# A planner's table of durations, the closing branch, the flags and the last output of a fused scan and dense kernel

## The chip, the cores and the metric

The kernel runs on one core of a Trainium2 chip. The time is device microseconds of that core, from launch to end. A core has five engines with a queue of instructions each: TensorE (PE, matrix products), VectorE (DVE), ScalarE (ACT), GpSimd (POOL) and SyncE (SP, which here issues nearly all transfers). Each engine does its instructions in order; between engines they wait for one another by semaphores.

## What is computed

A gated linear scan per head, and behind it a dense layer with a smooth gate:

```python
mag = np.sqrt(a_re * a_re + a_im * a_im)
scale = np.minimum(mag, 0.999) / (mag + 1e-06)
a_re_n, a_im_n = (a_re * scale, a_im * scale)
for t in range(S):
    new_re = ar * S_re - ai * S_im
    new_im = ar * S_im + ai * S_re
    S_re, S_im = (new_re + kv, new_im)          # kv = k[t] v[t]^T
    y[:, :, t] = np.einsum('bhd,bhde->bhe', q[:, :, t], S_re)
...
h = x @ w_in                                    # x = y as 3072 tokens x 384
g = np.where(pos, h, np.where(neg, 0.0, (h + beta) ** 2 / (4.0 * beta)))
return (g @ w_out).astype(np.float32)
```

There are 4 batches, 8 heads, 768 steps and a head size of 48 in float32; w_in is 384 x 2048, w_out 2048 x 384.

## The kernel before

The 3072 tokens are cut into 12 units of 256, and the units into 6 blocks of 2. For each unit, `gates(u)` turns the gate inputs into running sums, logarithms, angles and exponentials (DVE and ACT, with triangular sums on PE in the head of the program), and multiplies them into x (for q) and kq (for k). `spread` moves these into the tiles hd by DMAs on SP (pieces of 288, 128 and 32 KB). `attend(u)` then does the scan as chunked attention on PE: scores, transposes, values and products, bundled in visits, with DVE copying masked scores into am and ACT copying results. Results go to xr, with small moves from partition to partition (`move`, 16 KB). `split(blk)` makes a high part xH (ACT) and a low part xL (DVE) of x.

`moe(blk)` does the dense layer of 512 tokens: for each of 16 slices f of the hidden size a `gemm1` (h, 9 matmuls of 128x512: three groups of three) and a `gemm2` (9 matmuls into the three outputs o, again three groups). Between them s (ACT), g (DVE), gh (ACT, a rounded copy) and gl (DVE, the rest) are made of h. In the trace o's three banks are o_112, o_113 and o_114. At a block's end ACT copies o to ob, and SP sends it.

The weights come in a coded form (raw_i, raw_o) and are decoded by `weights`: integer operations on DVE (y_i, y_o, raw_i, raw_o), casts on ACT, and for the first ones a pair of matmuls (rest) on PE. The fast path is valid only within bounds of the inputs, so `slopes` and `ranges` (tiles far and chk) accumulate checks on ACT; in the last block these are 32 operations of 128x768 on chk.

No order is written by hand. All of this are operations of a `Plan`, each with an engine, a planned duration, what it reads and writes, and for some a due time. `Plan.order` simulates the engines with those durations (and LAT, the hand-over between engines; DMA_FIX and a rate for transfers; LANES transfers at a time) and picks for each engine what goes next; the program has that order on each engine. `emit(warm)` puts idle matmuls (L1293) on PE where the plan has PE waiting before the dense layer begins.

After the planned part, written by hand: DVE reduces the accumulated checks to flags (L1334 to L1342), PE adds them over the partitions (L1346), DVE makes `ok` of them (L1348, L1350), every engine loads `ok` into a register (L1353), and a branch on it (L1354) leaves out a slow path for inputs outside of the bounds. The code of that path lies between the branch and the end of the program.

## Time and profile before

| what | value |
|---|---|
| median of 3 runs | 576.93 us (575.53 to 577.64) |
| the profiled execution, time | 578.44 us |
| the profiled execution, span | 576.7 us |
| mean granted clock of PE | 0.994 |
| first matmul of the dense layer | 69.05 us |
| last matmul of the dense layer starts | 568.76 us |

The span runs from the first to the last instruction of the profile, and all times below are microseconds from its start. Busy is the time in which an engine executes; an arrow in a row names what an engine waited for, with the us of idle time before it. Rows whose engine ends in q show the sequencer's own instructions (branches, register loads, issues of DMAs), which aren't counted as busy. PE's granted clock is 1.00 at full rate.

### The profile page before, as it was taken

The numbers are of one execution on the slowest core, as the hardware profiler recorded it, in microseconds if no ns is written. First come the engines' busy times: TensorE is split into PE (matmuls) and PEld (weight loads), VectorE is DVE, ScalarE is ACT, GpSimd is POOL, SyncE is SP. The second block draws the span as 40 slices with busy tenths as digits, with TensorE's granted clock in tenths as the row PEclk, the third lists the DMA queues.
The fourth block names the chain that finished last, engine by engine and source line by source line (L and its number), as shares of the span: only waits on it lengthen the run. The fifth ranks groups of instructions, "written<-read, shape, count | busy, mean of one in ns | idle before, by whom it ended". The sixth has DMA issues, their size and how long they took to land.

```text
span 576.7 us, 10719 instructions
## 1 busy us (share of the span) xinstructions
PE 560.3 (97%) x4284; PEld 466.6 (81%) x4284; DVE 438.9 (76%) x610; ACT 391.0 (68%) x636; POOL 4.1 (1%) x27
## 2 busy tenths in 40 slices
PE   8999889999999999999999999999999999999994
PEld 8788768878888888888888888888887888888883
DVE  6999889899969998887887878887666644454453
ACT  7777678988975857776667486666355543369972
POOL 2000000000000000000000000000000000000000
PEclk9999989999999999999999999999999999999998
DMA  8678371863541602614403414403553500087721
GB/s 352 277 209 265 110 243 60 254 228 109 159 166 42 200 27 57 211 56 117 150 2 101 167 56 117 151 2 90 179 165 97 171 1 8 19 308 254 258 92 61
DMA packets 23673, 80.59 MB, mean 140 GB/s; under 512 B 4544, under 2 KB 10304, under 8 KB 23616
## 3 DMA queue, kind: packets, MB, share of 16 engines
q1 hardware_dynamic: 23616, 79.84, 41.7%
q8 instruction: 35, 0.57, 0.4%
q14 instruction: 22, 0.18, 0.1%
HBM read 55.05 MB, written 4.72 MB: 104 GB/s over the span
## 4 chain that ended last, share of the span: by engine, by line
PE 75%; DVE 11%; DMA 5%; ACT 4%; issue 2%; SPq 1%; ACTq 0%; DVEq 0%
PE h L1165 29%; PE o L1240 29%; PE at L992 5%; PE at L1044 3%; PE at L1036 3%; PE at L961 2%; DMA far<-in_ari_dram 2%; PE at L932 2%; ACT ai L626 2%; SPq L420 1%; DVE x L836 1%; DMA raw_i<-in_wl_dram 1%; DVE kq L836 1%; DVE raw_i L458 1%; DMA ai<-in_art_dram 1%
## 5 line engine op out<-in xcount | busy, mean ns | idle before, releaser
L1165 PE MATMUL h<-xH,wi 128*128 128x512 f32 x576 | 181.3, 396 | 4.5 <-DVE g L1209 3.0
L1240 PE MATMUL o<-gh,wo 128*128 128x512 f32 x576 | 180.2, 394 | 0.0
L1165 PEld LDWEIGHTS h<-xH,wi 128*128 128x128 f32 x576 | 105.9, 188 | 27.7 <-DVE g L1209 3.8
L1240 PEld LDWEIGHTS o<-gh,wo 128*128 128x128 f32 x576 | 106.3, 188 | 22.2 <-issue 0.3
L1165 PE MATMUL h<-xL,wi 128*128 128x512 f32 x288 | 112.8, 392 | 0.4 <-DVE xL L1142 0.4
L1240 PE MATMUL o<-gl,wo 128*128 128x512 f32 x288 | 112.4, 390 | 0.0
L1209 DVE TENSOR_TENSOR g<-h,s 128x512 f32<-128x512 f32 x96 | 65.9, 686 | 56.3 <-ACT s L1190 44.6
L1223 ACT CAST gh<-g 128x512 fp32r<-128x512 f32 x96 | 59.3, 617 | 53.3 <-DVE g L1217 51.0
L1190 ACT ACTIVATE s<-h,cst 128x512 f32<-128x512 f32 x96 | 65.5, 683 | 38.2 <-PE h L1165 35.6
L1227 DVE TENSOR_TENSOR gl<-g,gh 128x512 fp32r<-128x512 f32 x96 | 65.8, 686 | 32.8 <-ACT gh L1223 32.4
L1165 PEld LDWEIGHTS h<-xL,wi 128*128 128x128 f32 x288 | 54.2, 188 | 12.8 <-DVE xL L1142 1.1
L1240 PEld LDWEIGHTS o<-gl,wo 128*128 128x128 f32 x288 | 54.1, 188 | 11.8 <-DVE gl L1227 0.2
L1217 DVE SCALAR_TENSOR_TENSOR g<-s,g 128x512 f32<-128x512 f32 x80 | 55.3, 691 | 2.3
L626 ACT ACTIVATE ai<-ai 128x768 f32<-128x768 f32 x48 | 40.3, 843 | 20.1 <-DMA ai<-in_ari_dram 8.8
L992 PEld LDWEIGHTS at<-hd 96*64 96x64 f32 x704 | 33.2, 140 | 7.8 <-issue 6.3
L992 PE MATMUL at<-hd 96*64 96x64 f32 (+1 forms) x704 | 37.1, 255 | 0.0
L701 DVE TENSOR_TENSOR_SCAN ai<-again,ai 128x768 f32<-128x768 uint8 x20 | 35.0, 1751 | 0.3
L1044 PE MATMUL at<-am,V 128*64 128x128 f32 x352 | 32.9, 273 | 0.0
L1004 DVE COPY_PREDICATED am<-tri,at 128x512 f32<-128x512 uint32 x44 | 31.6, 737 | 1.6 <-PE at L992 1.6
L1036 PE MATMUL at<-hd,st 96*64 96x128 f32 x304 | 30.5, 278 | 0.3 <-DVE am L1004 0.3
L1293 PE MATMUL idle<-tri,ident 128*128 128x128 f32 x204 | 27.1, 292 | 1.8 <-POOL tri masks.py:66 1.8
L1293 PEld LDWEIGHTS idle<-tri,ident 128*128 128x128 f32 x204 | 26.3, 208 | 2.7 <-POOL tri masks.py:66 1.8
(124 smaller groups left out, 643.3 us busy)
## 6 DMA issues: line engine op xcount, KB each, us to landing
chk<-in_wl_dram SPq DMA_DIRECT2D x16, 768.0 KB, 6.4
kq<-in_kq_dram SPq DMA_DIRECT2D x12, 768.0 KB, 5.8
ai<-in_ari_dram SPq DMA_DIRECT2D x10, 768.0 KB, 6.2
V<-in_v_dram SPq DMA_DIRECT2D x12, 576.0 KB, 4.1
hd<-x SPq DMA_DIRECT2D x24, 288.0 KB, 3.7
hd<-kq SPq DMA_DIRECT2D x24, 288.0 KB, 4.0
raw_i<-in_wl_dram SPq DMA_DIRECT2D x8, 768.0 KB, 7.0
raw_o<-in_wl_dram SPq DMA_DIRECT2D x8, 768.0 KB, 4.7
```

The source lines that it names most:

```text
L626: lambda: A_.activation(out(), src(), f, **kw),
L992: PE_.matmul(SC.get()[o : o + HC, i + e, HC * k :], t[:, 0, ks], t[:, 1, qs], start=True, stop=True,)
L1036: PE_.matmul(o_, st.get().rearrange("p h e -> p (h e)")[:, lo : lo + 64], head(h)[:, 1, cs], start=True, stop=False,)
L1044: PE_.matmul(o_, V.get()[:, c, lo : lo + 64], ams[pr // 2].get()[:, 2 * (pr % 2) + e, :], start=st is None, stop=True,)
L1165: PE_.matmul(H.get(), weight["i", f // 2].get()[:, f % 2, part, sl], x.get()[:, j, :], start=j == 0 and n == 0, stop=j == NJ - 1 and n == 2,)
L1190: lambda: A_.activation(SS.get(), H.get(), AF.Relu, bias=c_half, scale=-0.5 if spare else 0.5),
L1209: lambda: V_.tensor_tensor(G.get(), H.get(), SS.get(), op=ALU.max),
L1217: lambda: V_.scalar_tensor_tensor(G.get(), SS.get(), 1.0, G.get(), op0=ALU.min, op1=ALU.mult),
L1223: pl.op("ACT", act(T), lambda: A_.copy(GH.get(), G.get()), r=[G], w=[GH])
L1227: lambda: V_.tensor_tensor(GL.get(), G.get(), GH.get().bitcast(F32), op=ALU.subtract),
L1240: PE_.matmul(PO[m].get(), weight["o", f // 2].get()[:, f % 2, part, sl], g.get(), start=f == 0 and n == 0, stop=f == NF - 1 and n == 2,)
L1293: PE_.matmul(idle["h1"], ident, mask, start=True, stop=True)
```

## The change

Four things are changed.

*The planner's table.* Transfers have a little less fixed cost; moves between tiles have constants of their own and a duration by size in place of a rate; transposes, products, scores and values have other planned durations; 400 ns at the head of a values visit go, and the last part of a visit has 300 or 100 ns added in place of 90. Nothing computed changes by it, but the order of the operations does, on every engine.

*The end of the last block.* With `BACK = 3`, gemm2 of f = 13, 14 and 15 is held back in the last block and done output by output, and gemm1 of f = 15 is due 0.6 of a step earlier. The last output, m = 2, is copied in two halves of 256 columns, one by ACT and one by DVE, and sent by two transfers, one on ACT's queue and one on SP's.

*Flags.* They become planned operations: they are on DVE as soon as all operations that accumulate checks (`marks`) are done, PE's sum stands ahead of o of f = 13, and `ok` is made ahead of gl of f = 15. The register loads of SP, ACT, DVE and POOL are planned as well and stand ahead of the last output's copies and transfers; PE's comes last. `nc.snap` replaces `nc.values_load` and does without two small instructions on SP (FUSED_REGOPS and SEQ_ASSERT).

*The branch.* `mark_branch_hint_location` puts one BRANCH_PREFETCH_HINT at the beginning of every engine's program, which names the closing branch and says that it is likely taken.

```diff
-DMA_FIX, DMA_END, DMA_ISSUE, LANES = 2400, 50, 470, 8
-LOAD, MOVE = 410.0, 240.0
+DMA_FIX, DMA_END, DMA_ISSUE, LANES = 2350, 50, 440, 8
+MOVE_FIX, MOVE_ISSUE = 1750, 605
+LOAD = 410.0
+MOVE = {16: 180, 32: 185, 128: 360, 288: 1330}
...
+BACK = 3
...
-                own = DMA_FIX + DMA_END + dma + 600
+                own = self.fix[i] + DMA_END + dma + 600
...
-                q.append(max(t + DMA_FIX, q[-1]) + dma)
+                q.append(max(t + self.fix[i], q[-1]) + dma)
...
+QUEUES = {
+    mybir.EngineType.SP: "SP",
+    mybir.EngineType.Activation: "ACT",
+    mybir.EngineType.DVE: "DVE",
+    mybir.EngineType.Pool: "POOL",
+}
...
-    def dma(nbytes, dst, src, r=(), w=(), due=None, rate=LOAD, eng="SP", after=()):
+    def dma(nbytes, dst, src, r=(), w=(), due=None, move=False, eng="SP", after=()):
         queue = {"SP": nc.sync, "ACT": nc.scalar, "POOL": nc.gpsimd}[eng]
         return pl.op(
             eng,
-            DMA_ISSUE,
+            MOVE_ISSUE if move else DMA_ISSUE,
             lambda: queue.dma_start(dst(), src()),
             r=r,
             w=w,
-            dma=nbytes / rate,
+            dma=MOVE[nbytes // 1024] if move else nbytes / LOAD,
             due=due,
             after=after,
+            fix=MOVE_FIX if move else DMA_FIX,
         )
...
+    def mark(*args, **kw):
+        marks.append(pl.op(*args, **kw))
...
-        pl.op(
+        mark(
             "ACT",
             act(N, acc=True) + 50,
             lambda: A_.activation(
...
-            ve(80, lambda: V_.tensor_copy(dst, A()[:, :, U - 1]), [a], [STATE[0]])
+            marks.append(ve(80, lambda: V_.tensor_copy(dst, A()[:, :, U - 1]), [a], [STATE[0]]))
...
-                out.append((4 * 83, run, [hd[h // 3] for h in GROUPS[g]], TP, tail))
+                out.append((4 * 76, run, [hd[h // 3] for h in GROUPS[g]], TP, tail))
...
-            return [(NH * 124, run, [*kT, V_c[0]], DP, tail)]
+            return [(NH * 114, run, [*kT, V_c[0]], DP, tail)]
...
-                out.append((2 * 340, run, [hd[h // 3] for h in GROUPS[g]], SC, tail))
+                out.append((2 * 345, run, [hd[h // 3] for h in GROUPS[g]], SC, tail))
...
-                return ((4 if st else 2) * len(prs) * 110 + (400 if prs[0] == 0 else 0), run, r, Y, tail)
+                return ((4 if st else 2) * len(prs) * 113, run, r, Y, tail)
...
+            mode = not 300 < parts[0][0] < 310
             last = None
             for n, (cost, run, r, psum, tail) in enumerate(parts):
-                cost += 90 if n == len(parts) - 1 else 0
+                if n == len(parts) - 1:
+                    cost += 300 if mode else 100
...
-                    due=t0 + STEP * (f + j / 6),
+                    due=t0 + STEP * (f + j / 6 - 0.6 * (f + 1 == NF and held_back > 0)),
...
+            gated.append(i)
+
+        def gemm2(f, ms=range(NJ), late=0.0):
+            GH, GL = gs[f]
+            for m in ms:
...
+                    due=t0 + STEP * (f + LAG - 0.5 + late + m / 6),
...
+        held_back = BACK if blk == NBLK - 1 else 0
         for k in range(NF + LAG):
             if k < NF:
                 gemm1(k)
-            if k >= LAG:
+            if LAG <= k < NF + LAG - held_back:
                 gemm2(k - LAG)
+        for m in range(NJ if held_back else 0):
+            for f in range(NF - held_back, NF):
+                gemm2(f, (m,), NF - f - 1 + (m * held_back + f) / 9)
...
+            due = t0 + STEP * (NF + LAG + 1.5)
+            ends = blk == NBLK - 1 and m == NJ - 1
+            for n, eng in enumerate(("ACT", "DVE") if ends else ("ACT",)):
+                sl = slice(n * U, (n + 1) * U) if ends else slice(0, T)
+                us = BLOCKS[blk][n : n + 1] if ends else BLOCKS[blk]
+                slot = "y" if n else turn_of("s", 3)
+                OB = tl(slot, [P, sl.stop - sl.start], F32, f"ob_{blk}_{m}_{n}")
+                copy = A_.copy if eng == "ACT" else V_.tensor_copy
+                i = pl.op(
+                    eng,
+                    act(sl.stop - sl.start, psum=True),
+                    lambda m=m, OB=OB, sl=sl, copy=copy: copy(OB.get(), PO[m].get()[:, sl]),
+                    r=[PO[m]],
+                    w=[OB],
+                    due=due,
+                )
+                if blk < NBLK - 1:
+                    finals.append(i)
+                dma(
+                    P * (sl.stop - sl.start) * 4,
+                    lambda m=m, us=us: out[PLACE[us[0]] : PLACE[us[-1]] + 1 : NPART, m].rearrange(
+                        "n p t -> p n t"
+                    ),
+                    lambda OB=OB: OB.get().rearrange("p (n t) -> p n t", t=U),
+                    r=[OB],
+                    due=due + STEP / 2,
+                    eng="ACT" if ends and n == 0 else "SP",
+                )
...
+    for fn in (
+        lambda: V_.tensor_scalar(fsum[:, 0], fsum[:, 0], SUM, None, op0=ALU.is_le),
...
+        lambda: V_.tensor_reduce(ok4[:, 3:4], wall, axis=AX.X, op=ALU.min),
+    ):
+        pl.op("DVE", 150, fn, w=[OK], after=marks, due=BEGIN[NBLK])
+    pl.op("PE", 190, lambda: PE_.matmul(FP.get(), ones, ok4, start=True, stop=True), r=[OK], w=[FP])
+    pl.op("DVE", 150, lambda: V_.tensor_reduce(ft, FP.get(), axis=AX.X, op=ALU.add), r=[FP], w=[OK])
+    pl.op(
+        "DVE",
+        150,
+        lambda: V_.tensor_scalar(ok, ft, 4.0 * P, None, op0=ALU.is_equal),
+        w=[OK],
+    )
+    for reg in regs:
+        if reg.engine in QUEUES:
+            pl.op(
+                QUEUES[reg.engine],
+                1000,
+                lambda reg=reg: nc.reg_load(reg, ok[0:1, 0:1]),
+                r=[OK],
+                after=[gated[-1]],
+                due=BEGIN[NBLK],
+            )
+
     with tc.manual_schedule():
+        tc.mark_branch_hint_location("general", "LikelyTaken", engines=mybir.ALL_ENGINES)
         pl.emit(warm)
-
...
+        for reg in regs:
+            if reg.engine not in QUEUES:
+                nc.reg_load(reg, ok[0:1, 0:1])
     fast.close()
 
-    within = nc.values_load(ok[0:1, 0:1], min_val=0, max_val=1)
-    with tc.If(within == 0):
+    within = nc.snap(regs, donate=True, min_val=0, max_val=1)
+    with tc.If(within == 0, label="general"):
```

How the order moves, at three places. (A number behind a tile's name counts the program's tiles; before and after, the same tile has another number.)

DVE in the head, where the products with kq of the first two units (kq_129 and kq_137) are made; raw_i_141 and raw_o_257 are weights. Before:

```order
L836 TENSOR_TENSOR x_139<-kq_129,ai_124 128x1536
L788 TENSOR_SCALAR state<-ai_126 128x3
L836 TENSOR_TENSOR kq_129<-kq_129,ai_124 128x1536
L458 SCALAR_TENSOR_TENSOR raw_i_141<-raw_i_141,y_i_294 128x768
L836 TENSOR_TENSOR x_146<-kq_137,ai_126 128x1536
L467 SCALAR_TENSOR_TENSOR raw_i_141<-raw_i_141 128x768
L836 TENSOR_TENSOR kq_137<-kq_137,ai_126 128x1536
L449 TENSOR_SCALAR y_o_382<-raw_o_257 128x768
L458 SCALAR_TENSOR_TENSOR raw_o_257<-raw_o_257,y_o_382 128x768
```

After, the same weights are raw_i_149 and raw_o_248; the four products (L852 now) come four rows and more behind these:

```order
L462 TENSOR_SCALAR y_i_290<-raw_i_149 128x768
L471 SCALAR_TENSOR_TENSOR raw_i_149<-raw_i_149,y_i_290 128x768
L480 SCALAR_TENSOR_TENSOR raw_i_149<-raw_i_149 128x768
L771 TENSOR_SCALAR ai_132<-o_114 128x512
L779 SCALAR_TENSOR_TENSOR ai_132<-o_114,ai_132 128x512
L771 TENSOR_SCALAR ai_132<-at_111 128x256
L779 SCALAR_TENSOR_TENSOR ai_132<-at_111,ai_132 128x256
L804 TENSOR_SCALAR state<-ai_132 128x3
L462 TENSOR_SCALAR y_o_317<-raw_o_248 128x768
```

The integer work on raw_i_149 and the first operation on the next weight (y_o) stand ahead of the products, rather than among and behind them.

DVE at the first h of the dense layer: x_342 and kq_492 are the products of unit 2, xL_681 the low part that the first h reads, and wo, y_i and raw_i weights. Before:

```order
L836 TENSOR_TENSOR x_342<-kq_492,ai_144 128x1536
L1142 TENSOR_TENSOR xL_681<-xr_467,xH_675 128x256
L836 TENSOR_TENSOR kq_492<-kq_492,ai_144 128x1536
L1142 TENSOR_TENSOR xL_681<-xr_467,xH_675 128x256 x2
L640 TENSOR_TENSOR ai_499<-ai_499 128x768
L478 TENSOR_TENSOR wo_753<-raw_o_534,wo_753 128x2x384
L449 TENSOR_SCALAR y_i_774<-raw_i_584 128x768
L458 SCALAR_TENSOR_TENSOR raw_i_584<-raw_i_584,y_i_774 128x768
L467 SCALAR_TENSOR_TENSOR raw_i_584<-raw_i_584 128x768
L1209 TENSOR_TENSOR g_0_792<-h_0_737,s_0_776 128x512
```

After (kq_512, xL_682; x_361 stands just ahead of it):

```order
L852 TENSOR_TENSOR kq_512<-kq_512,ai_152 128x1536
L1161 TENSOR_TENSOR xL_682<-xr_488,xH_671 128x256 x2
L989 TENSOR_TENSOR st_647<-st_647,o_112 96x384
L1161 TENSOR_TENSOR xL_682<-xr_488,xH_671 128x256
L656 TENSOR_TENSOR ai_518<-ai_518 128x768
L480 SCALAR_TENSOR_TENSOR raw_i_530<-raw_i_530 128x768
L1228 TENSOR_TENSOR g_0_806<-h_0_765,s_0_793 128x512
```

Of the four operations on weights between xL and the first g (L1209, now L1228) one is left there, and all of xL comes behind the product kq.

PE at the end of the program, from the first o on that reads gh of f = 14 (before) and of f = 15 (after). Before:

```order
L1240 MATMUL o_112<-gh_14_5293,wo_1574 128x512 x2
L1240 MATMUL o_112<-gl_14_5298,wo_1574 128x512
L1240 MATMUL o_113<-gh_14_5293,wo_1574 128x512 x2
L1240 MATMUL o_113<-gl_14_5298,wo_1574 128x512
L1240 MATMUL o_114<-gh_14_5293,wo_1574 128x512 x2
L1240 MATMUL o_114<-gl_14_5298,wo_1574 128x512
L1240 MATMUL o_112<-gh_15_5320,wo_1574 128x512 x2
L1240 MATMUL o_112<-gl_15_5325,wo_1574 128x512
L1240 MATMUL o_113<-gh_15_5320,wo_1574 128x512 x2
L1240 MATMUL o_113<-gl_15_5325,wo_1574 128x512
L1240 MATMUL o_114<-gh_15_5320,wo_1574 128x512 x2
L1240 MATMUL o_114<-gl_15_5325,wo_1574 128x512
```

After, where gh_13_5286, gh_14_5315 and gh_15_5338 belong to f = 13, 14 and 15:

```order
L1260 MATMUL o_112<-gh_15_5338,wo_1602 128x512 x2
L1260 MATMUL o_112<-gl_15_5344,wo_1602 128x512
L1260 MATMUL o_113<-gh_14_5315,wo_1602 128x512 x2
L1260 MATMUL o_113<-gl_14_5322,wo_1602 128x512
L1260 MATMUL o_113<-gh_15_5338,wo_1602 128x512 x2
L1260 MATMUL o_113<-gl_15_5344,wo_1602 128x512
L1260 MATMUL o_114<-gh_13_5286,wo_1514 128x512 x2
L1260 MATMUL o_114<-gl_13_5294,wo_1514 128x512
L1260 MATMUL o_114<-gh_14_5315,wo_1602 128x512 x2
L1260 MATMUL o_114<-gl_14_5322,wo_1602 128x512
L1260 MATMUL o_114<-gh_15_5338,wo_1602 128x512 x2
L1260 MATMUL o_114<-gl_15_5344,wo_1602 128x512
```

Six groups of three follow from the first o of f = 15 on, rather than three, and the last three groups all go into one output.

More of the change, by code (lines that the diff above doesn't have):

```diff
@@ L137, in tile, with op @@
         return t
-    def op(self, eng, cost, fn, r=(), w=(), due=None, dma=0, after=(), glue=None):
+    def op(self, eng, cost, fn, r=(), w=(), due=None, dma=0, after=(), glue=None, fix=DMA_FIX):
         i = len(self.ops)
@@ L526, in ranges @@
         )
-        pl.op(
+        mark(
             "ACT",
@@ L622, in ac @@
             cost = act(N, ptr=not isinstance(kw.get("bias", 0.0), float), acc=acc_ is not None)
-            pl.op(
+            (pl.op if acc_ is None else mark)(
                 "ACT",
@@ L855, in spread @@
                     r=[t],
-                    rate=MOVE,
+                    move=True,
                     eng=eng,
@@ L865, in spread @@
                     r=[t],
-                    rate=MOVE,
+                    move=True,
                     eng=eng,
@@ L876, in spread @@
                         r=[t],
-                    rate=MOVE,
+                    move=True,
                     eng=eng,
@@ L1075, in move @@
                     r=[(XR, (x, ub * U + q * CH)) for q in range(NC) for x in (False, True)],
+                    move=True,
                     w=[(XR, (ub, e, j))],
@@ L1231, in gemm1 @@
             gs[f] = (GH, GL)
-        def gemm2(f):
-            GH, GL = gs.pop(f)
-            for m in range(NJ):
+            gated.append(i)
+        def gemm2(f, ms=range(NJ), late=0.0):
+            GH, GL = gs[f]
+            for m in ms:
                 def mms(m=m):
@@ L1325, in gated_scan_moe @@
         moe(blk)
+    ok4 = const.tile([P, 4], F32, name="ok4")
+    ft = const.tile([1, 1], F32, name="ft")
+    ok = const.tile([1, 1], mybir.dt.int32, name="ok")
+    regs = nc.alloc_registers("within", engines=mybir.ALL_ENGINES)
+    wall = wsum.rearrange("p a b -> p (a b)")
+    decs = fdec.rearrange("p a b -> p (a b)")
+    OK, FP = fixed(ok4), tl("at0", [1, 4], F32, "fp")
+    for fn in (
+        lambda: V_.tensor_scalar(fsum[:, 0], fsum[:, 0], SUM, None, op0=ALU.is_le),
+        lambda: V_.tensor_reduce(ok4[:, 0:1], fsum[:, 0], axis=AX.X, op=ALU.min),
+        lambda: V_.tensor_scalar(fsum[:, 1], fsum[:, 1], FOURTH, None, op0=ALU.is_le),
+        lambda: V_.tensor_reduce(ok4[:, 1:2], fsum[:, 1], axis=AX.X, op=ALU.min),
+        lambda: V_.tensor_scalar(decs, decs, DECAY, None, op0=ALU.is_lt),
+        lambda: V_.tensor_reduce(ok4[:, 2:3], decs, axis=AX.X, op=ALU.min),
+        lambda: V_.tensor_scalar(wsum[:, 0], wsum[:, 0], T_SUM, None, op0=ALU.is_le),
+        lambda: V_.tensor_scalar(wsum[:, 1], wsum[:, 1], 0.0, None, op0=ALU.is_le),
+        lambda: V_.tensor_reduce(ok4[:, 3:4], wall, axis=AX.X, op=ALU.min),
+    ):
+        pl.op("DVE", 150, fn, w=[OK], after=marks, due=BEGIN[NBLK])
```

50 lines of the change are left out of this document (7 added, 43 removed).

## The prediction

> **What bounds the kernel now.** I read the page first, then the waits of PE, the busy time by stretches, and the timeline of the last 20 us. Page: the busy time of the engines, and the shares of the chain that ended last.
>
> ```profile
> span 576.7 us, 10719 instructions
> ...
> PE 560.3 (97%) x4284; PEld 466.6 (81%) x4284; DVE 438.9 (76%) x610; ACT 391.0 (68%) x636; POOL 4.1 (1%) x27
> ...
> PE 75%; DVE 11%; DMA 5%; ACT 4%; issue 2%; SPq 1%; ACTq 0%; DVEq 0%
> ```
>
> PE is busy for 97% of the span, so only idle time of PE, work added to it, and the time before its first and after its last useful matmul can move the end. Busy time by stretches (from:to, length, then each engine's busy us):
>
> ```profile
> 60.00:80.00 20.00, 15.49 (x136) 12.39 (x135) 17.16 (x24) 15.78 (x26) 0.00 (x0) 0.96 0.49 149
> 100.00:560.00 460.00, 459.30 (x3306) 380.31 (x3305) 345.35 (x474) 310.54 (x516) 0.00 (x0) 1.00 0.39 126
> ```
>
> From 100 to 560 us PE lacks 0.7 us of being full: a better order can gain no more than that there, though it can lose. What is left lies at three places: the head (before the dense layer's first matmul at 69.05), the turn from 60 to 80 us, where 20.00 - 15.49 = 4.5 us of PE are idle, and the end. The two largest waits of PE that the change can reach, the nearest row for a wait on attention, and the timeline of the first and third h:
>
> ```profile
> PE h L1165 <- DVE g L1209: 3.0, 2, 2.6
> PE h L1165 <- ACT xH L1135: 1.6, 1, 1.6
> PE at L1036 <- DVE am L1004: 0.3, 1, 0.3
> ```
> ```profile
> 69.05 0.73 PE L1165 MATMUL h<-xH,wi 128*128 128x512 f32 x2 [1.59 <-ACT xH L1135]
> ...
> 76.85 0.73 PE L1165 MATMUL h<-xH,wi 128*128 128x512 f32 x2 [2.58 <-DVE g L1209]
> ```
>
> **The end** is the largest term. Timeline of the last matmuls and outputs, the issues of the output's transfers (KB each, us to landing), and the instructions of the closing branch (count, shortest/median/longest in ns, first and last start):
>
> ```profile
> 566.25 0.69 DVE L1227 TENSOR_TENSOR gl<-g,gh 128x512 fp32r<-128x512 f32 x1 [0.69 <-ACT gh L1223]
> ...
> 566.86 0.17 DVE L1334 TENSOR_SCALAR fsum<-fsum 128x12 f32<-128x12 f32 x1
> ...
> 567.40 0.39 PE L1240 MATMUL o<-gl,wo 128*128 128x512 f32 x1
> ...
> 567.88 1.89 ACT L1267 COPY ob<-o 128x512 f32<-128x512 f32 x3 [1.67 <-PE o L1240]
> ...
> 568.50 1.67 SPq L420 DMA_DIRECT2D out_dram<-ob  x3
> ...
> 568.76 0.39 PE L1240 MATMUL o<-gl,wo 128*128 128x512 f32 x1
> ```
> ```profile
> out_dram<-ob SPq DMA_DIRECT2D x3, 256.0 KB, 2.3
> ```
> ```profile
> L1353 PEldq TENSOR_LOAD <-ok x1: 603/603/603, 569.7 to 569.7; - x1
> ```
> ```profile
> L1354 SPq EVENT_SEMAPHORE  x8: 17/17/17, 574.8 to 575.3; - x8
> L1354 ACTq COMPARE_BRANCH  x1: 50/50/50, 570.2 to 570.2; - x1
> L1354 POOLq COMPARE_BRANCH  x1: 45/45/45, 570.4 to 570.4; - x1
> L1354 PEldq COMPARE_BRANCH  x1: 4744/4744/4744, 570.4 to 570.4; - x1
> ...
> L1354 POOLq EVENT_SEMAPHORE  x1: 17/17/17, 570.8 to 570.8; - x1
> ...
> L1354 ACTq EVENT_SEMAPHORE  x1: 17/17/17, 574.3 to 574.3; - x1
> ```
>
> The last matmul starts at 568.76 and the span ends at 576.7: 7.9 us. The branch over the fallback is where they go. POOL is past it in 0.4 us (570.4 to 570.8); ACT needs 4.1 (570.2 to 574.3), PE 4.7. The page counts 27 instructions on POOL and 610 to 4284 on the others, so I read the 4 us as the fetch of code that is not at hand, where POOL's still is. If the announcement makes it there, every engine is past in POOL's 0.4 us, and the last output decides: its copy begins 0.4 us after the last matmul's start (three copies of 0.63 end at 567.88 + 1.89 = 569.77, the last begins at 569.14); half a copy takes 0.3 to 0.6, I take 0.4, its transfer starts at once and lands 2.3 later, so 568.76 + 0.4 + 0.4 + 2.3 = 571.9. Behind it stand the closing waits, 574.8 to 576.7 = 1.9 us; about half of them need not wait for the landing. The end is then 572.8 to 573.8, I take 573.2: **-3.5 us** (bounds -2.9 and -3.9). The early flags and register loads are in it: with them nothing but the output is late, and without the flags the 0.6 us of the load would stand in front of PE's branch. If the branch still fetches, PE's load and branch begin 0.6 us earlier and nothing else: -0.6.
>
> [...]
>
> **The last block's order.** ACT and DVE make one pair gh, gl per 2.7 us there, and the first can't be earlier, since ACT goes from its checks straight to s of f = 13:
>
> ```profile
> 557.05 1.00 ACT L530 ACTIVATE chk<-chk,cst 128x768 f32<-128x768 f32 x1
> ...
> 558.04 0.66 ACT L1190 ACTIVATE s<-h,cst 128x512 f32<-128x512 f32 x1
> 560.19 0.62 ACT L1223 CAST gh<-g 128x512 fp32r<-128x512 f32 x1 [1.48 <-DVE g L1217]
> 560.71 0.68 ACT L1190 ACTIVATE s<-h,cst 128x512 f32<-128x512 f32 x1
> ```
>
> gl of f = 15 ends at 566.25 + 0.69 = 566.94, and the matmul that first reads it stands at 567.40, a slack of 0.46 us. Now six groups rather than three follow from o0 of f = 15 on. A group of three matmuls takes 0.68 us (567.40 to 568.76 is two of them), so that PE comes there 3 x 0.68 = 2.04 us sooner, though gl comes no sooner: it waits 2.04 - 0.46 = 1.6 us. Nine flag operations like the fsum row (0.17 us) now stand among g and gl on DVE, mostly in gaps like the 0.69 of the gl row; with the flag's matmul on PE I add 0.1. **+1.7 us**, bounds +0.5 (ACT done with its checks a us sooner) and +2.3 (all flag work on the chain).
>
> **The head.** DVE, where it now has the weights' integer work ahead of the attention's, and PE's first groups:
>
> ```profile
> 9.86:32.31 22.45, 20.82 (x31) 1.00 0.74 296
> ...
> 67.57:76.19 8.62, 8.55 (x12) 1.00 0.61 174
> ```
> ```profile
> 32.31 1.76 DVE L836 TENSOR_TENSOR kq<-kq,ai 128x1536 f32<-128x1536 f32 x1
> 33.99 0.95 DVE L458 SCALAR_TENSOR_TENSOR raw_i<-raw_i,y_i 128x768 uint32<-128x768 uint32 x1
> ...
> 36.52 0.95 DVE L467 SCALAR_TENSOR_TENSOR raw_i<-raw_i 128x768 uint32<-128x768 uint32 x1
> ...
> 39.06 0.56 DVE L449 TENSOR_SCALAR y_o<-raw_o 128x768 uint32<-128x768 uint32 x1
> ...
> 69.57 1.75 DVE L836 TENSOR_TENSOR kq<-kq,ai 128x1536 f32<-128x1536 f32 x1
> ```
>
> The second to fourth row pass the product that ends kq of the first unit (32.31): 0.95 + 0.95 + 0.56 = 2.5 us more ahead of it. DVE idles 22.45 - 20.82 = 1.6 us before it, and about 1 of that is filled, since the weights' loads also go ahead of kq on SP. So the first scores come 1.5 us later. Up to the first g DVE does the same set of work in both orders, and is then without a gap (8.55 of 8.62); what was moved ahead is not done behind. The third h, which waits for that g, is therefore 0 to 1.5 us later; I take **+1.0**. The hint as second instruction of SP adds at most 0.1, in the bounds.
>
> **The middle** is local: a visit of attention goes ahead of or behind one group of the dense layer. With 0.7 us to gain and more to lose, **+0.5**, bounds -0.7 and +2.
>
> **The clock.** Windows of 3.41 us laid on the edges of the half-clock stretch: length, PE busy, granted clock:
>
> ```profile
> 68.12:71.53 3.41, 2.31 (x8) 1.00 0.36 98
> ...
> 74.95:78.36 3.41, 1.51 (x7) 1.00 0.74 181
> 78.36:81.77 3.41, 3.41 (x30) 0.50 0.96 387
> ```
>
> One stretch with PE busy for 1.51 of 3.41 us cost the next one half its clock, 1.7 us of work; 2.31 did not. The new order puts the second product of unit 2 (the 1.75 us at 69.57) ahead of all of xL rather than behind its first piece, so that the first h comes 1.0 + 1.75 = 2.75 us later where the third is only 1.0 later, and the wait of 2.58 at the third h shrinks to 0.8 at least; I take 1.4, since the wait for xL inside the first two h goes as well. That leaves 2.0 busy in any such stretch, between the two rows and nearer to the upper; where a stretch's edge falls inside the wait it is more. I take the dip to be gone: **-1.7**, bound 0.
>
> **Sum.** -3.5 + 1.7 + 1.0 + 0.5 - 1.7 = -2.0 us. The profiled execution took 578.44 (its span is 576.7), which is 1.5 above the median of the runs, 576.93; the difference is taken off the median: **574.9 us**. 0.5%, or 2.9 us, is about what a measurement of this kernel can tell from no change, so that "faster" begins below 574.0.
>
> **Rivals.**
> 1. Good ends: the tail's wait is short (+0.5), head and middle cost nothing, the dip goes: -3.5 + 0.5 - 1.7 = -4.7, 572.2 us. For it: DVE's total in the head is unchanged. Against: the slack of 0.46 before six groups. Chance 0.26.
> 2. The announcement does nothing and the branch still fetches: -0.6 in place of -3.5, 577.8 us, no change. For it: it stands hundreds of instructions ahead of the branch. Against: only the not yet fetched code explains 4.1 against 0.4 us. Chance 0.13.
> 3. Slower: the attention's values now come too early. For a visit that begins with values the planner held 400 + 90 ns beyond its matmuls and now holds 300, so that what follows is fitted in closer; PE runs in order, so that a visit whose masked scores are not yet copied stops everything behind it.
>
> ```profile
> L1004 DVE COPY_PREDICATED am<-tri,at x44: 706/736/762, 42.3 to 477.8; 128x512 f32<-128x512 uint32 x44
> ```
>
> Two copies a visit, with the four into another bank, are 24 visits. A wait of 0.3 us (the one in the row of waits) at each is 7 us: 574.9 + 7 = 582. It turns the sign at 576.93 - 574.9 = 2.0 us, 0.08 a visit, and is slower by over 0.5% from 4.9 us, 0.2 a visit. Against: groups of the dense layer that don't depend on them stand between most of these, and the waits of PE have one single wait for am in the whole run. Chance 0.11.
>
> **Chances.** My forecast 0.5, the rivals 0.26, 0.13, 0.11. Faster by over 0.5%: the first rival and the lower edge of my own case, 0.34. Slower: 0.11. Same: 0.55. The range goes from the first rival, 572.0, past the second to 579.0; beyond are most of the third and a little below.
>
> **What would show it.** Branch: ACT's and PE's next instruction within 0.6 us of theirs, and 4 to 5 us from the last matmul to the end; a PE branch of over 4 us is rival 2. Tail: a new wait of PE for gl or g of 1 to 2 us in the last 15 us. Head: first h at 70 to 72 us, its third f about 1 us later than 76.85. Clock: no stretch at 0.50 after 70 us. Middle: under 2 us of PE idle from 100 to 560; many waits for am there is rival 3. I am wrong if the head is earlier, or if the last output's landing takes well over 3 us.

## The result, and the profile after

| kernel | median | runs | ratio to before, 95% interval |
|---|---|---|---|
| before | 578.12 us (575.53 to 579.61) | 8 | |
| after | 580.91 us (579.21 to 584.88) | 8 | 1.0052 [1.003, 1.0074] |

The changed kernel is slower by 0.5%; 574.9 us were predicted, with 572.0 to 579.0 as range. The forecast stood on a median of three runs for before, 576.93; with eight it is 578.12, so that 1.2 us of the 6.0 between 574.9 and 580.91 belong to the baseline: as a change, -2.0 us were forecast and +2.8 measured. The profiled execution of after took 579.93 us (span 578.1) against 578.44 (span 576.7), so that the profile shows about half of the difference; the other half is looked for in the profiles of the experiments.

The page of after, and the busy time by stretches (from:to, length, busy us of PE, PEld, DVE, ACT and POOL, granted clock, DMA share, GB/s), and below them the row of before for 100 to 200 us:

```profile
span 578.1 us, 10750 instructions
...
PE 561.2 (97%) x4300; PEld 466.0 (81%) x4300; DVE 439.1 (76%) x611; ACT 391.2 (68%) x636; POOL 4.1 (1%) x27
```
```profile
60.00:80.00 20.00, 17.53 (x185) 14.95 (x181) 16.59 (x24) 15.22 (x25) 0.00 (x0) 1.00 0.48 135
100.00:200.00 100.00, 96.42 (x707) 78.74 (x706) 88.06 (x117) 80.24 (x123) 0.00 (x0) 1.00 0.49 152
100.00:560.00 460.00, 456.30 (x3288) 377.12 (x3287) 343.21 (x473) 309.30 (x514) 0.00 (x0) 1.00 0.39 125
```
```profile
100.00:200.00 100.00, 99.69 (x727) 82.42 (x726) 90.89 (x122) 83.82 (x129) 0.00 (x0) 1.00 0.51 162
```

From 60 to 80 us PE is busy for 17.53 us where it was 15.49, but that is hardly progress: 0.9 us of it is idle matmuls (5.59, was 4.70), and a step of the attention ahead of the dense layer (the transposes with ident) comes 2.0 us later (61.00, was 58.97), so that more of it falls into this stretch. What is better is the clock: before ran at half of it for 3.4 us from 78.4 on, after does not. The middle is worse: 460.00 - 456.30 = 3.7 us of PE idle from 100 to 560, where it was 0.7, and nearly all of it between 100 and 200 us. PE's waits, and the third h in the timeline:

```profile
PE h L1184 <- DVE g L1228: 3.7, 4, 1.7
...
PE at L948 <- DVE am L1020: 1.2, 2, 0.8
PE o L948 <- DVE am L1020: 1.0, 1, 1.0
```
```profile
76.89 0.73 PE L1184 MATMUL h<-xH,wi 128*128 128x512 f32 x2 [1.75 <-DVE g L1228]
...
117.15 0.74 PE L1184 MATMUL h<-xH,wi 128*128 128x512 f32 x2 [0.48 <-DVE g L1228]
...
122.31 0.73 PE L1184 MATMUL h<-xH,wi 128*128 128x512 f32 x2 [0.75 <-DVE g L1228]
...
128.13 0.55 PE L948 MATMUL at<-ident,hd 96*128 96x96 f32 x4 [0.76 <-DVE am L1020]
...
161.61 1.52 PE L1008 MATMUL at<-hd 96*64 96x128 f32 x30 [0.89 <-DMA hd<-kq]
...
179.42 0.73 PE L1184 MATMUL h<-xH,wi 128*128 128x512 f32 x2 [0.71 <-DVE g L1228]
```

The third h comes when it did (76.89, was 76.85), after a shorter wait. The new waits are five: for g at 117, 122 and 179 us, for am at 128, and for a move (hd<-kq) at 161.6; they make 3.6 us. What holds g at 117 and 122 us is on DVE. First before, then after, the timeline of DVE (in brackets the idle time ahead and what ended it), and SP's issues in after:

```profile
112.83 0.95 DVE L640 TENSOR_TENSOR ai<-ai 128x768 f32<-128x768 f32 x1
115.61 0.56 DVE L449 TENSOR_SCALAR y_i<-raw_i 128x768 uint32<-128x768 uint32 x1 [1.83 <-DMA raw_i<-in_wl_dram]
116.09 0.68 DVE L1209 TENSOR_TENSOR g<-h,s 128x512 f32<-128x512 f32 x1
```
```profile
111.32 0.95 DVE L656 TENSOR_TENSOR ai<-ai 128x768 f32<-128x768 f32 x1
115.93 0.56 DVE L462 TENSOR_SCALAR y_i<-raw_i 128x768 uint32<-128x768 uint32 x1 [3.66 <-DMA raw_i<-in_wl_dram]
116.41 0.69 DVE L1228 TENSOR_TENSOR g<-h,s 128x512 f32<-128x512 f32 x1
```
```profile
103.84 1.80 SPq L432 DMA_DIRECT2D hd<-x  x3
105.74 0.68 SPq L432 DMA_DIRECT2D hd<-kq  x1
107.10 0.35 SPq L447 DMA_DIRECT2D raw_i<-in_wl_dram  x1
107.51 1.16 SPq L432 DMA_DIRECT2D hd<-kq  x2
```

In both kernels the decoding of a weight (y_i) stands ahead of g on DVE, and the weight lands at nearly the same time, 115.6 and 115.9. In after the s that g reads is done on ACT at 112.70 (112.07 + 0.63), and g starts at 116.41, right behind y_i, though DVE idled for 3.66 us. After is 1.5 us earlier there (ai at 111.32, was 112.83), which is about the 1.7 us that PE did not lose to a half clock at 78 us, and DVE waits 1.8 us longer: so much of a gain is given back at one load, and 1.2 us of it shows as idle PE at 117 and 122 us. The wait for am at 128 us follows the next weight in the same way (DVE waits 0.70 us for raw_o at 125.29). The other two, 1.6 us, do not stand behind a decoding: at 161.6 PE waits for a move itself, and the g of 179 us stands on DVE behind a product with kq (177.02 to 178.7). In after the load of 116 us, of 768 KB, is issued at 107.10 behind four moves and ahead of six, and lands after 8.8 us; in before it is issued at 108.96 behind six and ahead of four, and lands after 6.6. For a load with nothing queued ahead of it the planner holds 2350 + 768 x 1024 / 410 + 50 ns = 4.3 us.

The end. The closing branch (count, shortest/median/longest in ns, first and last start), the last two copies, the last transfers (KB, us to landing), and SP's closing semaphores:

```profile
L1404 PEldq COMPARE_BRANCH  x1: 391/391/391, 569.5 to 569.5; - x1
...
L1404 ACTq COMPARE_BRANCH  x1: 68/68/68, 573.6 to 573.6; - x1
...
L1404 ACTq EVENT_SEMAPHORE  x1: 17/17/17, 574.1 to 574.1; - x1
```
```profile
572.82 0.37 ACT L1298 COPY ob<-o 128x256 f32<-128x256 f32 x1 [1.41 <-PE o L1260]
...
573.23 0.42 DVE L1298 COPY ob<-o 128x256 f32<-128x256 f32 x1 [4.44 <-ACT ob L1298]
```
```profile
out_dram<-ob ACTq DMA_DIRECT2D x1, 128.0 KB, 2.0
out_dram<-ob SPq DMA_DIRECT2D x1, 128.0 KB, 2.9
```
```profile
L1635 SPq EVENT_SEMAPHORE  x10: 17/28/28, 576.8 to 578.1; - x10
```

The last matmul starts at 572.40 and the span ends at 578.1: 5.7 us, where it was 7.9. ACT is past its branch in 0.5 us (573.6 to 574.1). But the halves don't run beside each other: DVE's copy waits for ACT's (573.23 is behind 572.82 + 0.37), and its transfer is the one that lands last.

### The profile page after: what moved, and what is told of

Read it like the earlier page. It is cut to its first block, busy times and chain, and to the rows that moved or that the text cites. A ratio compares the mean times of both kernels' runs of the same rounds, so it can differ in the third digit from the quotient of the medians.

```text
span 578.1 us, 10750 instructions
## 1 busy us (share of the span) xinstructions
PE 561.2 (97%) x4300; PEld 466.0 (81%) x4300; DVE 439.1 (76%) x611; ACT 391.2 (68%) x636; POOL 4.1 (1%) x27
## 4 chain that ended last, share of the span: by engine, by line
PE 63%; DMA 15%; DVE 11%; ACT 8%; issue 2%; SPq 1%; ACTq 0%; DVEq 0%
PE o L1260 24%; PE h L1184 24%; PE at L1008 5%; DMA chk<-in_wl_dram 4%; PE at L1052 3%; PE at L1060 3%; DMA hd<-kq 2%; PE at L977 2%; ACT chk L546 2%; PE at L948 2%; DMA raw_i<-in_wl_dram 2%; DMA kq<-in_kq_dram 1%; SPq L432 1%; DMA out_dram<-ob 1%; DVE g L1228 1%
## 5 line engine op out<-in xcount | busy, mean ns | idle before, releaser
L1228 DVE TENSOR_TENSOR g<-h,s 128x512 f32<-128x512 f32 x96 | 66.0, 687 | 55.9 <-ACT s L1209 44.4
L1209 ACT ACTIVATE s<-h,cst 128x512 f32<-128x512 f32 x96 | 65.5, 682 | 38.8 <-PE h L1184 36.2
L1008 PE MATMUL at<-hd 96*64 96x128 f32 (+1 forms) x704 | 36.7, 251 | 0.9 <-DMA hd<-kq 0.9
```

Of the source, the lines that this page charges most:

```text
L1008: PE_.matmul(SC.get()[o : o + HC, i + e, HC * k :], t[:, 0, ks], t[:, 1, qs], start=True, stop=True,)
L1209: lambda: A_.activation(SS.get(), H.get(), AF.Relu, bias=c_half, scale=-0.5 if spare else 0.5),
L1228: lambda: V_.tensor_tensor(G.get(), H.get(), SS.get(), op=ALU.max),
```

## The experiments

Each kernel was timed in five rounds against before; ratios are to before.

**The branch.** e1 is before with the announcement alone, e2 is after without it.

```diff
 e1, on before:
+        tc.mark_branch_hint_location("general", "LikelyTaken", engines=mybir.ALL_ENGINES)
         pl.emit(warm)
-    with tc.If(within == 0):
+    with tc.If(within == 0, label="general"):
 e2, on after:
-        tc.mark_branch_hint_location("general", "LikelyTaken", engines=mybir.ALL_ENGINES)
```

> The kernel before, and of the change only the announcement of the branch. Theory A (the announcement works and is worth what the end shows): every engine's next instruction comes within 0.6 us of its branch, and the end is set by the third output's landing, 572.8 us in the trace of before, and 1.3 us of closing: 574.1, so 2.0 to 3.0 us faster than before. Rival B (the shorter end of the changed kernel comes from the early register loads and the early flags alone): branches of 3.4 to 4.7 us as before, no difference.

> The changed kernel without the announcement. Theory A: ACT's and SP's branches take 3.4 to 4.1 us again from 573.6 and 574.1 on, but the last landing at 576.6 hides most of it: 0.5 to 1.5 us slower than the changed kernel. Rival B: no difference from the changed kernel. Rival C (the announcement is worth the whole 4 us of the branch wherever it stands): 3 to 4 us slower.

e1: 0.9985 [0.9964, 1.0007]. e2: 1.0057 [1.003, 1.0083]. The branches in e1 and in e2:

```profile
L1355 ACTq COMPARE_BRANCH  x1: 68/68/68, 570.6 to 570.6; - x1
...
L1355 PEldq COMPARE_BRANCH  x1: 4824/4824/4824, 570.7 to 570.7; - x1
...
L1355 ACTq EVENT_SEMAPHORE  x1: 17/17/17, 571.0 to 571.0; - x1
```
```profile
L1403 PEldq COMPARE_BRANCH  x1: 3339/3339/3339, 572.3 to 572.3; - x1
...
L1403 ACTq COMPARE_BRANCH  x1: 54/54/54, 576.4 to 576.4; - x1
...
L1403 ACTq EVENT_SEMAPHORE  x1: 17/17/17, 579.7 to 579.7; - x1
```

The announcement works for ACT (0.4 us to be past in e1, 3.3 without it in e2). For PE it did nothing in e1: 4824 ns, so that the end came 7.4 us behind the last matmul's start (569.06, span 576.5) and the whole gain was out of reach. So theory A of e1 held for ACT and failed for PE, and its time is as rival B had it. From the last matmul to the end e2 takes 581.9 - 575.14 = 6.8 us: of the 2.2 us that the end gained, the announcement is 1.1 by these profiles, one of each kernel, and all else that changed there (early flags, early loads, halves) the other 1.1. The times of e2 and after (1.0057 and 1.0052) can't tell theory A of e2 from B; C is out.

**The table.** e3 is after with all old durations, e4 is before with all new ones.

```diff
 e3, on after:
-DMA_FIX, DMA_END, DMA_ISSUE, LANES = 2350, 50, 440, 8
-MOVE_FIX, MOVE_ISSUE = 1750, 605
+DMA_FIX, DMA_END, DMA_ISSUE, LANES = 2400, 50, 470, 8
+MOVE_FIX, MOVE_ISSUE = 2400, 470
-MOVE = {16: 180, 32: 185, 128: 360, 288: 1330}
+MOVE = {n: n * 1024 / (410.0 if n == 16 else 240.0) for n in (16, 32, 128, 288)}
...
-                    cost += 300 if mode else 100
+                    cost += 90
 e4, on before: the same lines the other way
```

> The changed kernel with the planner's old durations of transfers, moves and attention; new end, flags and announcement stay. Theory A (the new table costs 3.0 us of waits between 100 and 560 us and saves 1.7 us of half clock): no PE wait over 0.4 us between 100 and 540, half clock at about 78 us again, 1.3 us faster than the changed kernel in a like trace, 1 to 3 in the median. Rival D (all that was lost was lost at the end, by the held back gemm2): as slow as the changed kernel within 0.5 us.

> The kernel before with the new table alone; old end, old flags, no announcement. Theory A: PE waits of 3 us between 100 and 200 us, no half clock at 78, 1 to 3 us slower than before. Rival D: within 0.5 us of before.

e3: 0.9999 [0.9971, 1.0027]. e4: 1.0045 [1.0023, 1.0068]. The table alone makes before as slow as after; without it the rest of the change comes to nothing (in e3's profile the end takes 6.3 us where it was 7.9, but the last matmul starts 1.1 us later, at 569.90), much as theory A of both had it. e4's stretch has the same loss, and its waits are of the same kinds: g 3.9 us in four (1.72 of them at the third h), am 0.6 and, in the head, 1.8, and a move (hd<-kq) 1.0:

```profile
100.00:200.00 100.00, 96.17 (x703) 78.09 (x702) 87.54 (x117) 79.74 (x122) 0.00 (x0) 1.00 0.48 150
```

The profiles of e2 and e4 also show the half of the loss that the profile of after lacks. In e2, DVE and then PE in the head:

```profile
54.63 0.56 DVE L462 TENSOR_SCALAR y_o<-raw_o 128x768 uint32<-128x768 uint32 x1 [2.72 <-DMA raw_o<-in_wl_dram]
...
57.09 1.33 DVE L1020 COPY_PREDICATED am<-tri,o 128x512 f32<-128x512 uint32 x2
```
```profile
57.86 0.55 PE L948 MATMUL o<-ident,hd 96*128 96x96 f32 x4 [2.46 <-DVE am L1020]
...
79.31 0.73 PE L1184 MATMUL h<-xH,wi 128*128 128x512 f32 x2 [1.74 <-DVE g L1228]
```

It is the same pattern as at 116 us: a decode waits for its load, and am, queued behind it on DVE, keeps PE. In after's profile these waits are 1.39 and 1.0 us, and the third h 2.4 us earlier. In e2 the clock fell as well (0.70 from 58 to 61 us). So the missing half is probably the same wait in its longer form; that is not shown, since after has one profile, of one of its shorter executions.

**Moving the decoding.** In e5 the three DVE operations on the weight of 54 us are put 4 us later in the order, in e6 those of every weight from the sixth on.

```diff
+LATER = 4000
...
+        key = lambda i: (self.start[i] + self.later.get(i, 0.0), i)
...
 e5 (e6 has n >= 5):
+        if n == 6:
+            for j in range(len(pl.ops) - 3, len(pl.ops)):
+                pl.later[j] = LATER
```

> The changed kernel, with one weight's three integer operations on DVE (y_o and twice raw_o of the weight that is loaded at 48 us) put behind the masked copies am that followed them; nothing else moves on any engine. Theory A (in the head DVE stands in its order before that load, which lands 4.8 to 6.5 us after its issue where the planner holds 4.3, and PE waits for the copies behind): PE's wait of 1.0 to 2.5 us for am at 56 to 58 us goes, the third h comes 1 to 2 us earlier than the 76.9 to 79.3 seen with the new table, and the time is 0.5 to 2 us below the changed kernel's. Rival E (the sum of DVE's work up to the first g sets the third h): third h and time unchanged.

> The changed kernel, with the three integer operations of all weights from the sixth on put 4 us later in the order (operations that need them follow), so that loads have 4 us more to land. Theory A: DVE's waits for raw_i and raw_o (3.7 and 2.1 us) and PE's waits for g and am between 100 and 200 us (2.9 us) fall to under 1 us; 2 to 3 us below the changed kernel. Rival F (the later decoding is late for PE itself): PE waits for wi or wo, or for g behind the bunched integer work; no gain.

e5: 1.0068 [1.0044, 1.0093]. e6: 1.0294 [1.0259, 1.0329]. In e5 the wait only changed engines. ACT, and PE:

```profile
60.24 0.88 ACT L507 CAST wo<-raw_o 128x768 fp32r<-128x768 f32 x1 [2.73 <-DVE raw_o L498]
61.03 0.58 ACT L1093 COPY xr<-o 128x512 f32<-128x512 f32 x1
```
```profile
61.66 1.55 PE L1029 MATMUL o<-hd 96*64 96x128 f32 x16 [2.61 <-ACT xr L1093]
```

The cast of that weight stood on ACT ahead of a copy to xr, and kept its place. So e5 decides nothing on the head. In e6 g waits for the decoding everywhere (PE's waits for g are 9.3 us): a fixed delay of the decoding is no cure.

**The old table with parts of the rest.** e7 has the old table and the old order of the last block (BACK = 0); e8 has in addition the last output in one copy, and due times only on what makes the flags, none on the loads.

```diff
 e7 and e8, on after, with the lines of e3:
-BACK = 3
+BACK = 0
 e8 besides:
-            ends = blk == NBLK - 1 and m == NJ - 1
+            ends = False
...
                 after=[gated[-1]],
-                due=BEGIN[NBLK],
...
-        w=[OK],
+        w=[OK], due=BEGIN[NBLK],
```

> The changed kernel with the old table and without the held back gemm2 (BACK = 0); flags, loads, announcement and the two half copies stay. Theory A (the order by output makes PE wait for gh and gl of f = 15): the gaps of PE in the last 20 us, 1.3 us with the old table and BACK = 3, fall to 0.6 or less; 0.5 to 1 us faster than the run with the old table and BACK = 3. Rival G (the gaps come from the flags among g and gl on DVE): gaps stay over 1 us, no difference.

> Old table, gemm2 not held back, one copy and one transfer for the last output, announcement, early flags; the register loads planned without a due time, so that PE keeps the order of before but for the flags' matmul. Theory A: PE has one gap, 0.3 us at that matmul; its branch begins ahead of its last matmuls, so that the fetch is hidden; the span ends 5.2 to 6.0 us after the start of the last matmul where before needs 7.9: 1.5 to 2.5 us faster than before. Rival H (the landing of the last output and the closing waits set the end whatever the branch does): 7 us or more, within 1 us of before.

e7: 0.9991 [0.9966, 1.0015]. e8: 0.9963 [0.9941, 0.9985], faster than both kernels, though by little. e7 can't be told from e3 (0.9999), so that its time decides between neither of its expectations. e8's end takes 5.7 us (last matmul 571.16, span 576.9), in the range of its theory A, but not by a hidden branch: PE's took 3605 ns and was past only at 573.7.

**Which part of the table.** e9 has the old durations of transfers, e10 the old ones of attention; e11 has all of after's, but loads from DRAM 2350 ns dearer.

```diff
 e9: the lines of e3 on DMA_FIX, MOVE_FIX, MOVE
 e10: the lines of e3 on the attention (83, 124, 340, 110, 400, 90)
 e11:
-DMA_FIX, DMA_END, DMA_ISSUE, LANES = 2350, 50, 440, 8
+DMA_FIX, DMA_END, DMA_ISSUE, LANES = 4700, 50, 440, 8
```

> The kernel after with the durations of transfers as before (2400 ns plus bytes at 410 or 240 a ns, 470 to issue); the attention's new costs, the branch, flags, halves and last order stay. Theory A (the transfers' new prices are to blame: work that reads a load is placed earlier than the load lands, and what stands behind it on DVE waits with it): the loss from 100 to 200 us goes, PE busy there 99 to 100 of 100 us, ratio to before 1.000 (the kernel with the whole old table had 0.9999). Rival B (the attention's costs are to blame: its groups are placed earlier than their values): 96 to 97 us busy, ratio 1.005 as after.

> The kernel after with the attention's costs as before (83, 124, 340, 110 and the 400 and 90 behind a visit); the transfers' new durations and all else stay. Theory A: still 96 to 97 us of PE busy from 100 to 200, ratio to before 1.005. Rival B: 99 to 100 us busy, ratio 1.000. If both this and its counterpart with the old transfers lose nothing, neither half alone is to blame but how they meet in the order.

> The kernel after with one number changed: the fixed part of a load from DRAM 4700 in place of 2350 ns, so that a weight's piece of 768 KB is held for 6.7 us, about the middle of the 4.8 to 8.8 us that the trace of after shows for them. Theory A in its narrow form (it is the price of loads): DVE's wait for raw_i at 116 us goes to under 2 us, PE busy from 100 to 200 rises to 99 or more, ratio 1.001 or below. Rival: any further price only deals the order anew, or the moves' price is what counts: 96 to 98 us busy, ratio 1.003 to 1.01.

e9: 0.9929 [0.9902, 0.9956]. e10: 1.0055 [1.003, 1.0081]. e11: 0.9911 [0.9886, 0.9936]. The transfers are to blame, not the attention. e10 shows the late load at its plainest: DVE waits 5.07 us for raw_i until 116.27, and PE 4.3 us for the g behind it, with none of the other waits between 100 and 200 us. In e11 PE, and the load that was late in after:

```profile
100.00:200.00 100.00, 99.92 (x727) 82.42 (x726) 91.65 (x123) 83.93 (x128) 0.00 (x0) 1.00 0.50 158
```
```profile
104.06 0.33 SPq L447 DMA_DIRECT2D raw_i<-in_wl_dram  x1
109.69 2.59 SPq L432 DMA_DIRECT2D hd<-x  x4
```
```profile
112.44 0.56 DVE L462 TENSOR_SCALAR y_i<-raw_i 128x768 uint32<-128x768 uint32 x1
```

It is issued 3 us earlier and 5.6 us ahead of the moves instead of among them, and the decoding finds it there. Against before, e11's last matmul starts 2.0 us earlier (566.73, was 568.76), and its end takes 5.7 us in place of 7.9: the span is 572.4, was 576.7. e9's 0.9929 was lower than its expectation (1.000): with the old transfers, the new attention costs win 0.7% over e3's 0.9999.

**Which transfers.** The change made moves some 0.6 us cheaper and loads 0.05 us. e13 has only the moves' old price; e15 has dear loads and the old attention costs.

```diff
 e13, on after:
-MOVE_FIX, MOVE_ISSUE = 1750, 605
+MOVE_FIX, MOVE_ISSUE = 2400, 470
-MOVE = {16: 180, 32: 185, 128: 360, 288: 1330}
+MOVE = {n: n * 1024 / (410.0 if n == 16 else 240.0) for n in (16, 32, 128, 288)}
 e15: the lines of e10 and of e11
```

> The kernel after with only the moves' price as before (2400 ns fixed, bytes at 240 or 410 a ns, 470 to issue); the loads keep 2350 and 440. Theory A (moves priced some 0.6 us shorter let the planner start them, and so issue five of them, ahead of the weight's load, which then lands late): the loss goes as with all old transfers, 99 to 100 us of PE busy from 100 to 200, ratio to before 0.993. Rival (the loads' 50 ns count, or both together): 96 to 98 us busy, ratio 1.002 to 1.005.

> The kernel after with loads 2350 ns dearer and the attention's costs as before. Theory A (dear loads are enough: no load is late, and DVE's wait goes whatever the attention costs): 99 to 100 us of PE busy from 100 to 200, ratio to before 0.991 to 0.994. Rival (the attention's new costs are worth 0.7% by themselves, as between the kernels with old transfers, 0.9999 and 0.9929): 0.997 to 1.000, with a stretch of half clock after 70 us.

e13: 0.9918 [0.9888, 0.9948]. e15: 0.9898 [0.987, 0.9925]. The moves' price is what decides in after's table: putting it back takes off the whole loss and more. It isn't the price of moves by itself, though: e11 and e15 keep the new one, and dear loads take the loss off as well. How e13 does it differs from theory A. DVE in e13:

```profile
112.83 0.95 DVE L656 TENSOR_TENSOR ai<-ai 128x768 f32<-128x768 f32 x1
113.70 0.68 DVE L1228 TENSOR_TENSOR g<-h,s 128x512 f32<-128x512 f32 x1
114.30 0.95 DVE L491 TENSOR_TENSOR wo<-raw_o,wo 128x768 fp32r<-128x768 f32 x1
115.17 0.54 DVE L989 TENSOR_TENSOR st<-st,at 96x384 f32<-96x384 f32 x1
115.63 0.68 DVE L1246 TENSOR_TENSOR gl<-g,gh 128x512 fp32r<-128x512 f32 x1
116.89 0.56 DVE L462 TENSOR_SCALAR y_i<-raw_i 128x768 uint32<-128x768 uint32 x1 [0.57 <-DMA raw_i<-in_wl_dram]
```

The load is not earlier (issued at 110.48 behind eight moves, landed after 6.4 us at 116.9), but four operations, g among them, stand between ai and the decoding, and nothing urgent stands behind a late load. Dear loads cure it from the other side, by an earlier issue. Both keep what after lost.

**The two halves.** e12 is after with the last output in one copy, e14 the same with dear loads.

```diff
-            ends = blk == NBLK - 1 and m == NJ - 1
+            ends = False
```

> The kernel after with its last output in one copy and one transfer, all else as after. Theory (the two halves run one behind the other, since both read the same bank and the second waits for the first's semaphore, so that they save next to nothing): last matmul's start to the end 5.7 to 6.2 us, ratio to before 1.005 as after, within 0.1%. Rival (halves save what was predicted, half a copy and half a transfer, about 0.5 to 1 us): 6.2 to 6.7 us, ratio 1.006 to 1.007.

> The kernel after with loads 2350 ns dearer and the last output in one copy. Theory (the halves cost in the end, as one copy after them gave 0.4% in the interval's middle and 0.6 us in the profile): ratio to before 0.990 to 0.991, last matmul's start to the end 5.0 to 5.3 us against 5.7 of the one with halves. Rival (the halves are worth nothing either way and the 0.4% came from elsewhere): 0.991 to 0.993, 5.5 to 5.8 us.

e12: 1.0011 [0.9991, 1.0032], where after has 1.0052 [1.003, 1.0074]. e14: 0.9914 [0.9889, 0.9939], where e11 has 0.9911. In the profiles the end is shorter with one copy, 5.1 us (last matmul 571.58, span 576.7) against after's 5.7, and 4.9 (567.80, 572.7) against e11's 5.7 (566.73, 572.4). The profiles are close to what the theory of e14 had (5.0 to 5.3 against 5.7), and the times bear out a gain in the first pair, against both expectations of e12, and none in the second, as e14's rival had it. So the halves win nothing; whether they cost is open.

## Why the prediction was wrong

**The step that failed is "the middle is local", +0.5 us with +2 as its bound.** PE lost 3.0 us there, 3.7 in place of 0.7, and, as far as it was followed, it was not a matter of a visit going ahead of or behind a group: the order of loads, moves and decoding had changed, and those were coupled over many microseconds through SP's queue (the load of 116 us is issued 8.8 us ahead of its landing, among ten moves) and through DVE (the g of 116.41 stands behind the decoding for 3.7 us with its s done). No term and no rival had the prices of the transfers in it. I had looked at what the table does to PE's order and not at which DVE operation now stands behind which landing, though the row of before was in reach: 1.83 us of DVE idle at 115.61, with g behind it. e4 shows that the table alone does this, e13 that it goes when one part, the moves' price, is put back. Read off the traces alone is the way from the price to the waits: 2.0 of the 3.6 us stand behind late loads of weights, and what held the move at 161.6 us and the g at 179 us was not followed.

**The clock, -1.7.** In the profiled execution the stretch at half clock after 75 us is gone, as predicted, and so is its 1.7 us. The wait that was to shrink did, from 2.58 to 1.75 us (1.4 was taken), and the 17 profiles bear the link out: the twelve with 0.9 to 1.8 us of wait at the third h have no fall of the clock behind it, and of the five with 2.4 to 3.1 us three have one (before, e3, e15). But two have none (e1, 2.57 us, and e10, 3.05), and e1 has the order of before: so the 1.7 us is no steady loss of before, and its size rests on one execution. In e2, e4 and e14 the clock fell at 58 us or soon after instead (0.70, 0.54 and 0.55 granted from 57.97 to 61.38). The step also took for granted that an earlier PE stays earlier. At 116 us DVE waited for a landing that was no earlier (115.9, was 115.6). With the moves' old price the gain was kept: e9 and e13 have no such stretch either, and PE is busy for 100.00 us of 100 to 200 in both. And e15 has such a stretch (granted clock 0.81 and 0.69 from 75 to 82 us) and is no slower than e11 and e13, so that the fall by itself doesn't tell these kernels apart.

**The end, -3.5, bounds -2.9 and -3.9: measured -2.2.** ACT's part held: it is past the announced branch in 0.5 us, where it was 4.1, and the last output decides. The size was off in the last output's part. That half a copy takes 0.4 us and "its transfer starts at once" holds for ACT's half alone; DVE's copy starts 0.41 us later, and its transfer landed after 2.9 us and not 2.3. The closing semaphores behind the landing take 1.3 us (576.8 to 578.1), what the term had for them. That the two halves are copied at the same time was my assumption: in after the program makes DVE's copy wait for ACT's (4.44 us of idle time, ended by ACT's ob), and no run here has the two side by side. And one thing was not in the term: PE's own branch stayed slow in e1 though announced, 4824 ns; in after it took 391.

**The last block's order, +1.7 (bounds +0.5 and +2.3).** In after PE's weight loads show waits where they were predicted, at the flag's sum ("issue": the profile shows nothing that it waited for) and for gh and gl of f = 15:

```profile
565.53 0.09 PEld L1376 LDWEIGHTS at<-ok,cst 128*1 128x1 f32 x2 [0.35 <-issue]
568.11 0.30 PEld L1260 LDWEIGHTS o<-gh,wo 128*128 128x128 f32 x2 [0.55 <-ACT gh L1242]
568.84 0.19 PEld L1260 LDWEIGHTS o<-gl,wo 128*128 128x128 f32 x1 [0.43 <-DVE gl L1246]
```

They add up to 1.3 us, but weight loads overlap with matmuls (PEld is busy for 81% of the span and PE for 97%). By the matmuls, nine groups of three take 7.19 us in after (their last ones start at 565.21 and 572.40), where they would take 6.12 at 0.68 each: PE lost 1.1 us, below the term and within its bounds. It is no fixed price of this order: e11, with the same three outputs at the end, has only the first of the three waits (0.35 us at 560.58).

**The head, +1.0.** The attention's step before the dense layer came 2.0 us later (1.5 was forecast), the first h 1.1 us later (70.14, was 69.05; 2.75 was forecast), the third h 0.04 us later in the profile of after and 2.5 in e2's. The term lies between, but one profile of a kernel can't show it: e1, with the order of before, has its third h at 78.05, and the kernels with the old table spread from 76.85 to 78.78, after and e2 from 76.89 to 79.31. The hint on SP takes 56 ns in after.

**The account of the profile.** From the third h on, after's last matmul is 3.6 us later: -1.7 for the clock, +3.0 in the middle and +1.1 in the tail make 2.4; the last 1.2 us I can't assign. With the end's -2.2 the span is 1.4 us longer. The sum of the terms was -2.0: the middle missed by +2.5 us and the end by +1.3, the head and the tail by -1.0 and -0.6 the other way.

**The rivals.** The second (the announcement does nothing) is refuted for ACT, which is past its branch in 0.4 us in e1 and 0.5 in after, against 4.1 in before and 3.3 in e2, and stands for PE in four kernels (3605 to 4824 ns though announced; 4744 in before). That a slow branch spends its time on fetching code was my reading of the instruction counts; no row of any run shows what the engine does meanwhile. The third (slower, since attention's values come too early) had the sign right and the cause wrong: PE's waits for am are 2.2 us in three places, not a little at each visit, and e10, with the old attention costs, is as slow as after. The first (good ends, -4.7 us) has about the size of what e11, e13 and e15 gained: 574.4, 575.8 and 575.3 us, which is 5.0, 4.2 and 4.7 us, or 0.8 to 1.0%, under before in the same rounds.

Not settled: why the attention's new costs win 0.7% beside the old transfers (e3 to e9; 0.7 us of these 4 us is the end, 6.3 in e3 and 5.6 in e9) and nothing beside the dear loads (e15, e11) or the new transfers (e10, after), and how much of all these differences is one order's luck at a few places rather than a better price. e11, e13 and e15 can't be told apart; any of them is faster than both kernels.

## What to carry to other kernels

New durations in a planner's table made this kernel slower (1.0045 in e4), though nothing computed changed. The load of 116 us stood among moves in before, in after and in e13; what changed is how many stood ahead of it and behind it, when it was issued, and what waited behind it on DVE. The moves' new price is also no truer than the old one: for 288 KB the planner now holds 1750 + 1330 + 50 ns = 3.1 us and held 3.7, and in before the median was 3.7 (hd<-x) and 4.0 us (hd<-kq) from issue to landing; at 128 KB the planner now holds 2.2 us and held 3.0, and the medians in before were 3.7 and 3.9; at 32 KB 2.0 and 2.6, for 3.1 and 2.7; at 16 KB 2.0 and 2.5, for 2.6. The two kernels that price a transfer nearer to what it took in company, e13 the moves and e11 the loads, are 0.8 and 0.9% faster than before; how much of that is luck of the order is open. So price a transfer by what it takes in company, and look, in the trace of before, for the engine that idles ahead of a landing (here DVE, 1.83 us at 115.61) and for what its order has behind that operation (here g): there a gain made earlier was lost, 1.5 us at ai and none at the landing.
